# Second layer's first product over pairs of token blocks in 7 block products, with streamed weights and a planned order of instructions

## The chip, the cores and the metric

The kernel runs on one core of one Trainium2 chip, as one launch. The metric is the device time of that launch in microseconds (us), lower is better. Runs of the kernel before: 1168.96 us median of 3 (1168.02 to 1169.71). Five engines work side by side, each through its own instructions in order: TensorE (PE: matmuls, with weight loads as PEld), VectorE (DVE), ScalarE (ACT), GpSimd (POOL) and SyncE (SP, which here only issues DMAs). They wait for each other by semaphores.

## What is computed

Windowed attention gives 3072 tokens x 512 (6 blocks of 512 tokens), then two feed-forward layers follow. With x of shape (3072, 512):

```python
# first layer, d_ff = 1536
gate = 1.0 / (1.0 + np.exp(-(x @ w_gate)))
x = (gate * (x @ w_val)) @ w_out
# second layer, d_ff = 2048
h = x @ w_in
P = a[0] + a[1] * h + a[2] * h**2 + a[3] * h**3
Q = 1.0 + abs(b[0]) * abs(h) + abs(b[1]) * h**2
out = (P / (Q + 1e-06)) @ w_out
```

All data are 32-bit floats. The kernel keeps accuracy by splitting each operand into a high and a low part and adding three matmuls (high-high, high-low, low-high; `TERMS`), so each product of tiles costs three matmuls per 128 rows of contraction. The reciprocal of Q is made as the square of an inverse square root and corrected once.

## The kernel before

**First layer.** The attention of later blocks, the conversion of weights and the first layer are interleaved by a table of steps (`plan`, filled by `at`, run by `runner`). Blocks 0 and 1 take the gate and value products tile by tile (L373). Blocks 2, 3 and blocks 4, 5 are taken as pairs: `quads` calls `quad` (L490), which forms the products of a 2 x 2 arrangement (two blocks, two tiles of features) from 7 block products instead of 8, with differences and sums of x and of the weights made beforehand. Between the quads stand visits (`visit`, `out1`, L575), the products with w_out of an earlier tile; `outs` does the visits of the second block of a pair, whose results were held.

**Conversion.** The weights come as 64-bit words, are staged, decoded by two ScalarE and one VectorE instructions, and split into a high part (ScalarE, L345) and a low part (VectorE, L349). The 32 tiles of the second layer (16 of w_in, 16 of w_out, 512 KB each when split) are converted during the first layer; 28 are stored to HBM and loaded again before the second layer, 4 stay (`DIRECT`). In the second layer all of them are resident.

**Second layer.** For each of 6 blocks and each of 16 tiles f of 128 features: `h2` makes h for 512 tokens (12 matmuls of 512 columns, L618) into one PSUM bank, and then the rational function works on 512-wide tiles; `out2` adds the tile's share to the four accumulators of the block five steps later (12 matmuls, L657):

```python
        nc.scalar.activation(out=t, in_=hp, func=ACTF.Identity, scale=cf[:, 3:4], bias=cf[:, 2:3])
        nc.scalar.activation(out=qq, in_=hp, func=ACTF.Abs, scale=cab[:, 0:1])
        nc.scalar.activation(out=hh, in_=hp, func=ACTF.Square)
        nc.vector.tensor_tensor(out=t, in0=t, in1=hp, op=ALU.mult)
        nc.vector.scalar_tensor_tensor(out=t, in0=t, scalar=cf[:, 1:2], in1=hp, op0=ALU.add, op1=ALU.mult)
        nc.vector.scalar_tensor_tensor(out=qq, in0=hh, scalar=cab[:, 1:2], in1=qq, op0=ALU.mult, op1=ALU.add)
```

`recip2` (two ScalarE instructions, L638 and L639), `ratio2` (three VectorE, L644 to L646) and `split2` (one ScalarE, one VectorE, L560 and L561) follow, one or two steps later. `load_x2` and `split_x2` bring the next block's x from HBM, where the first layer stored it. The order on each engine is the program's, written out in a loop over `steps2`. The first three `h2` run between the last visits of the first layer.

**Buffers.** PSUM has four accumulator banks and four others (`ps`). In SBUF: 20 slots `w` and 8 slots `b` for weights and operands, 4 `x`, 4 `g`, and 14 temporaries `t` of 512 columns.

## Time and profile before

| | before |
|---|---|
| median of the runs | 1168.96 us |
| the profiled execution, its own time | 1168.19 us |
| its span, first to last instruction | 1166.4 us |
| PE busy | 1150.4 us (99%) |
| DVE busy | 865.6 us (74%) |
| ACT busy | 709.3 us (61%) |
| POOL busy | 2.1 us (0%) |
| mean granted TensorE clock | 0.994 of full speed |

The profile is one execution, recorded by the hardware. A busy share is an average over stages with different limits, so a stage is read by itself. Matmuls overlap one another, so the mean duration of one is longer than the distance from one to the next; the same holds, less so, for VectorE and ScalarE. The chain of waits follows the work that ended last back to what released it. A DMA's time to landing is counted from its issue.

### The profile page before, as it was taken

How to read it: one execution, taken by the hardware profiler on the slowest of the kernel's cores; microseconds unless marked ns; L12 is line 12 of the kernel's file. 1: busy time of each engine (PE TensorE's matmuls, PEld its weight loads, DVE VectorE, ACT ScalarE, POOL GpSimd, SP SyncE). 2: the span in 40 equal slices, each digit the busy share in tenths (PEclk: the TensorE clock that was granted, in tenths of full speed). 3: DMA queues.
4: the chain of work that ended last, by engine and by line, in shares of the span. 5: the costliest groups of instructions: out<-in, count | busy, mean ns of one | idle time of the engine just before them, and what ended most of it. 6: DMA issues, size and time to landing. Idle time of an engine off the chain costs nothing.

```text
span 1166.4 us, 19936 instructions
## 1 busy us (share of the span) xinstructions
PE 1150.4 (99%) x7942; PEld 946.7 (81%) x7945; DVE 865.6 (74%) x1342; ACT 709.3 (61%) x1208; POOL 2.1 (0%) x15
## 2 busy tenths in 40 slices
PE   6999999999999999999999999999999999999998
PEld 4788788888888888888888888888888888888887
DVE  5778867874576646556555898898898898888886
ACT  4989566653433365433344876767767767767664
POOL 0000000000000000000000000000000000000000
PEclk8899999999999999999999999999999999999999
DMA  9889799987878668988867620100100100100101
GB/s 371 318 314 336 253 333 382 351 324 280 335 263 295 239 241 320 393 321 284 310 234 312 217 81 10 55 10 10 55 10 10 55 10 10 55 10 1 37 1 36
DMA packets 67356, 218.09 MB, mean 187 GB/s; under 512 B 7488, under 2 KB 7744, under 8 KB 67264
## 3 DMA queue, kind: packets, MB, share of 16 engines
q1 hardware_dynamic: 66688, 215.42, 50.6%
q8 instruction: 62, 1.02, 0.3%
q10 hardware_dynamic: 576, 1.41, 0.3%
q14 instruction: 30, 0.25, 0.1%
HBM read 161.22 MB, written 55.57 MB: 186 GB/s over the span
## 4 chain that ended last, share of the span: by engine, by line
PE 93%; ACT 3%; DMA 2%; DVE 1%; issue 1%; SPq 0%; ACTq 0%; DVEq 0%
PE acc L657 22%; PE h L618 22%; PE p L490 19%; PE acc L575 15%; PE h L373 10%; DMA st<-w_in 2%; PE xp L280 1%; PE sp L220 1%; PE xp L187 1%; PE tp L265 1%; ACT st L310 0%; DMA q<-q_in 0%; ACT st L311 0%; ACT wp L345 0%; PE sp L113 0%
## 5 line engine op out<-in xcount | busy, mean ns | idle before, releaser
L575 PE MATMUL acc<-g,wp 128*128 128x512 f32 x864 | 210.5, 393 | 0.6 <-ACT x2s L591 0.6
L657 PE MATMUL acc<-wp,g 128*128 128x512 f32 x792 | 189.4, 389 | 0.0
L575 PEld LDWEIGHTS acc<-g,wp 128*128 128x128 f32 x864 | 160.2, 188 | 34.9 <-ACT x2s L591 1.0
L657 PEld LDWEIGHTS acc<-wp,g 128*128 128x128 f32 x792 | 148.6, 188 | 30.9
L626 ACT ACTIVATE t<-h,cf 128x512 f32<-128x512 f32 x96 | 74.8, 779 | 148.3 <-PE h L618 148.3
L618 PE MATMUL h<-x,w 128*128 128x512 f32 x648 | 155.5, 389 | 0.0
L618 PEld LDWEIGHTS h<-x,w 128*128 128x128 f32 x648 | 121.6, 188 | 25.3
L373 PE MATMUL h<-x,wp 128*128 128x512 f32 x576 | 139.7, 396 | 2.1 <-ACT x L196 1.5
L490 PE MATMUL p<-b,wpq_s 128*128 128x512 f32 x576 | 138.5, 389 | 0.1
L373 PEld LDWEIGHTS h<-x,wp 128*128 128x128 f32 x576 | 108.9, 191 | 25.3 <-ACT x L196 1.6
L490 PEld LDWEIGHTS p<-b,wpq_s 128*128 128x128 f32 x576 | 108.0, 188 | 22.9 <-DVE v L504 0.5
L618 PE MATMUL h<-x,wp 128*128 128x512 f32 x504 | 121.1, 389 | 0.0
L618 PEld LDWEIGHTS h<-x,wp 128*128 128x128 f32 x504 | 94.6, 188 | 19.7
L629 DVE TENSOR_TENSOR t<-t,h 128x512 f32<-128x512 f32 x96 | 65.9, 686 | 55.4 <-ACT hh L628 54.0
L560 ACT ACTIVATE g<-sg 128x512 fp32r<-128x512 f32 x36 | 22.8, 632 | 104.8 <-DVE sg L520 66.2
L657 PE MATMUL acc<-w,g 128*128 128x512 f32 x360 | 86.5, 389 | 0.0
L657 PEld LDWEIGHTS acc<-w,g 128*128 128x128 f32 x360 | 67.6, 188 | 14.0
L630 DVE SCALAR_TENSOR_TENSOR t<-t,cf,h 128x512 f32<-128x512 f32 x96 | 71.8, 748 | 3.4
L490 PE MATMUL p<-x,wpq_a 128*128 128x512 f32 x288 | 73.2, 389 | 0.0
L631 DVE SCALAR_TENSOR_TENSOR qq<-hh,cab,qq 128x512 f32<-128x512 f32 x96 | 71.7, 747 | 0.0
L645 DVE SCALAR_TENSOR_TENSOR t<-t,cf,y 128x512 f32<-128x512 f32 x96 | 71.6, 746 | 0.0
L644 DVE SCALAR_TENSOR_TENSOR qq<-qq,y 128x512 f32<-128x512 f32 x96 | 65.8, 686 | 7.1 <-ACT y L639 7.1
(120 smaller groups left out, 1506.8 us busy)
## 6 DMA issues: line engine op xcount, KB each, us to landing
st<-w_in SPq DMA_DIRECT2D x62, 512.0 KB, 7.1
wp<-wqa SPq DMA_DIRECT2D x60, 512.0 KB, 7.1
wpq_s<-wqs SPq DMA_DIRECT2D x48, 512.0 KB, 7.5
wpq_a<-wqa SPq DMA_DIRECT2D x36, 512.0 KB, 6.5
wqa<-wp SPq DMA_DIRECT2D x30, 512.0 KB, 8.8
w2d<-wpw SPq DMA_DIRECT2D x28, 512.0 KB, 6.1
v<-v_in SPq DMA_DIRECT2D x24, 512.0 KB, 7.8
wqs<-wps SPq DMA_DIRECT2D x24, 512.0 KB, 5.3
```

The costliest lines, as they stand in the source:

```text
L373: nc.tensor.matmul(pt, lhsT=w[:, a, c : c + P], rhs=x[:, kt, b], start=(h == 0 and kt == 0 and i == 0), stop=(h == 1 and kt == 1 and i == 2),)
L490: nc.tensor.matmul(bank[n], lhsT=wt[:, a, c : c + P], rhs=x[:, kt, b], start=(i < 4 and kt == 0 and t == 0), stop=(kt == 1 and t == 2), sk ...
L560: nc.scalar.activation(out=t[:, 0, 0:n], in_=sg, func=ACTF.Copy)
L575: nc.tensor.matmul(acc[j][d], lhsT=w[:, a, d * P : (d + 1) * P], rhs=g[:, b], start=(f == 0 and i == 0), stop=(f == NF1 - 1 and i == 2),)
L618: nc.tensor.matmul(hp, lhsT=w[:, a, kt * P : (kt + 1) * P], rhs=x[kt // 2][:, kt % 2, b], start=(kt == 0 and i == 0), stop=(kt == KT - 1 a ...
L626: nc.scalar.activation(out=t, in_=hp, func=ACTF.Identity, scale=cf[:, 3:4], bias=cf[:, 2:3])
L629: nc.vector.tensor_tensor(out=t, in0=t, in1=hp, op=ALU.mult)
L630: nc.vector.scalar_tensor_tensor(out=t, in0=t, scalar=cf[:, 1:2], in1=hp, op0=ALU.add, op1=ALU.mult)
L631: nc.vector.scalar_tensor_tensor(out=qq, in0=hh, scalar=cab[:, 1:2], in1=qq, op0=ALU.mult, op1=ALU.add)
L644: nc.vector.scalar_tensor_tensor(out=qq, in0=qq, scalar=QC, in1=y, op0=ALU.add, op1=ALU.mult)
L645: nc.vector.scalar_tensor_tensor(out=t, in0=t, scalar=cf[:, 0:1], in1=y, op0=ALU.add, op1=ALU.mult)
L657: nc.tensor.matmul(acc[j][m], lhsT=g[:, a, m * P : (m + 1) * P], rhs=w[:, b], start=(f == 0 and i == 0), stop=(f == NF2 - 1 and i == 2),)
```

## The change

The second layer takes blocks in 3 pairs and tiles of features in 8 groups of two (`feats`). Per pair and group, 7 block products of 6 matmuls each (`quad2`, `product`, `POS2`) replace the 48 matmuls of four `h2`. The combinations of weights (`COMBS2`) are made during the first layer: 28 tiles of input weights are stored (to `wq2`) for the 16 before, and all 16 output tiles (to `w2o`); none stays resident. Each pair loads them again: per group four loads of input weights (three of 512 KB, one of 256 KB; `load2i`) and four of output weights (512 KB; `load2o`). x of the two blocks is loaded, combined and split into 7 operands (`x_ops`: per pair 8 loads, 8 differences, 14 high and 14 low parts).

The 7 products of a group gather in three PSUM banks: X (taken in turn from two banks), Y and Z. ScalarE copies X out four times as it grows, VectorE adds Y or Z to three of the copies. That gives h of the two tiles for the first block (`hs`) and for the second (`bs`, held in the `x` slots). The rational function (`activation`) runs in passes 1024 wide over the two tiles of a block: five ScalarE instructions each; for the first block (i = 0) six on VectorE, for the second (i = 1) five, its sum b1 h^2 + b0 |h| being made by an accumulating DMA that GpSimd issues, SBUF to SBUF, 512 KB (`q_sum`; `sb` is the square root of b1, made in `second_scalars`).

Visits (`visit2`, 12 matmuls each, as in `out2`) stand two in each group and 16 after the 8 groups of a pair. Accumulators and the banks of the groups change places from pair to pair. Before the first group stand 10 of the first layer's last 14 visits, the other 4 in the first groups' slots.

The order of the second layer comes from a planner in the source (`Plan`): each instruction is a task with an engine, a duration, a latency, and what it reads, writes and takes from the buffer pools. TensorE's tasks keep their order; each other engine takes, whenever it is free in the plan, the ready task with the earliest latest-start. The plan is then emitted as the program order of each engine (`emit`).

The temporaries `t` become 7 buffers of two halves, which come free when both halves are done. `AHEAD` is 3 for 4, `DIRECT` 0 for 4. In the first layer the conversion of second-layer weights stands at other steps (`conv_in`, `conv_out`), with 16 combinations (`comb2`).

The core of the diff:

```diff
-AHEAD = 4
-DIRECT = 4
+AHEAD = 3
+NQ = 8
+NPAIR2 = 3
+DIRECT = 0
+FORDER = [4 * (q // 2) + q % 2 + 2 * i for q in range(8) for i in range(2)]
...
-    tpool = ctx.enter_context(tc.tile_pool(name="t", bufs=14))
+    tpool = ctx.enter_context(tc.tile_pool(name="t", bufs=7))
...
+    def t2w(name):
+        return tpool.tile([P, 2, 512], F32, tag="t", name=name)
+
     def t2(name):
-        return tpool.tile([P, 512], F32, tag="t", name=name)
+        if spare:
+            return spare.pop()[:, 1]
+        t = t2w(name)
+        spare.append(t)
+        return t[:, 0]
...
+    XORDER = ("21", "11", "1", "3", "2", "4", "22")
+    POS2 = (("11", 0), ("21", 1), ("2", 0), ("3", 2), ("1", 0), ("22", 0), ("4", 2))
+
+    def feats(s):
+        f = 4 * (s // 2) + s % 2
+        return f, f + 2
...
+    class Plan:
+        SIZES = {"t": 7, "b": 8, "w": 20, "x": 4, "g": 4}
+        LAT = {"PE": 0.25, "ACT": 0.15, "DVE": 0.15, "POOL": 5.0, "SP": 5.5}
...
+                    for t in queue[:1] if e == "PE" else queue:
+                        if best and best.late <= t.late or e != "PE" and t.late > now - stall + t.window:
+                            continue
+                        if any(
+                            d.start is None or d.start + d.dur + d.lat * (d.eng != e or e != "PE") > now + 1e-9 for d in t.deps
+                        ):
+                            continue
...
+    COMBS2 = {}
+    items = []
+    for fp in range(NF2 // 4):
+        a0, a1, b0, b1 = range(4 * fp, 4 * fp + 4)
+        s0, s1, s2, s3 = (("s", fp, o) for o in range(4))
+        COMBS2[s0] = b0, b1, ALU.add
+        COMBS2[s1] = s0, a0, ALU.subtract
+        COMBS2[s2] = a0, b0, ALU.subtract
+        COMBS2[s3] = a1, s1, ALU.subtract
+        items += [
+            (b1, [(0, b1, fp, 6)], []),
+            (b0, [(0, s0, fp, 4)], [(0, b1)]),
+            (a0, [(0, a0, fp, 0), (0, s2, fp, 3), (1, s1, fp, 2)], [(0, b0), (1, s0), (1, a0), (1, s2)]),
+            (a1, [(0, a1, fp, 1), (0, s3, fp, 5)], [(0, a1), (0, s1), (0, s3)]),
+        ]
+    outs2 = [NF2 + f for f in FORDER]
+    conv_in = [S1 + 1 + i for i in range(4)] + [O1 + 1 + 3 * i for i in range(4)]
+    conv_in += [Q2 + i for i in (0, 1, 2, 3, 5, 6, 7, 8)]
+    conv_out = [4, 5, 7, 17, 19, 20, 22] + [S1 + i for i in range(5, 11)] + [O1 + 2, O1 + 8, Q2 + 4]
...
+        WIN = 11.0
+
+        def load2o(key, f):
+            buf(key, "w", lambda: wpool.tile([P, 2, 512], F32R, tag="w", name="_".join(map(str, key))))
+            t = task(SP, 0.1, lambda: nc.sync.dma_start(out=env[key].bitcast(F32), in_=w2o[f]), (), [key], (), [key], lat=6.0)
+            t.window = WIN
+
+        def load2i(p, s, i):
+            key, n = ("wi", p, s, i), 1 if i == 3 else 2
+            buf(key, "w", lambda: wpool.tile([P, 2, 2, 256], F32R, tag="w", name=f"wi{p}_{s}_{i}"))
+
+            def load():
+                nc.sync.dma_start(out=env[key][:, 0:n].bitcast(F32), in_=wq2[s // 2, s % 2, i, :, 0:n])
+
+            task(SP, 0.1, load, (), [key], (), [key], lat=6.0).window = WIN
...
+            for n, o in enumerate(XORDER):
+                src, dst = pure.get(o, ("xf", p, kt, o)), ("x2", p, o)
+                if o in subs:
+                    x0, x1 = subs[o]
+                    buf(src, "t", lambda src=src: t2("_".join(map(str, src))), 1)
+                    task(
+                        DVE,
+                        0.68,
+                        lambda src=src, x0=x0, x1=x1: tt(out=env[src], in0=env[x0], in1=env[x1], op=ALU.subtract),
+                        [x0, x1],
+                        [src],
+                        [x0, x1],
+                        [src],
+                    )
+                if kt == 0:
+                    buf(dst, "b", lambda dst=dst: b_tile("_".join(map(str, dst)), F32R, [P, 2, 2, 512]))
...
+        def activation(p, s, i):
+            h = (lambda: flat(h_ap(p, s))) if i == 0 else (lambda: flat(b_ap(p, s)))
+            hk = h_key(p, s) if i == 0 else b_key(p, s)
...
+            kt, kq, ku = ((x, p, s, i) for x in "tqu")
+            ky, chain = ku, ("chain", (s, p) if i == 0 else CH(s))
...
+            by_dma = QDMA(i)
+            scale = {"scale": sb[:, 0:1]} if by_dma else {}
+            task(
+                ACT,
+                0.97,
+                lambda: act(out=w(ku), in_=h(), func=ACTF.Square, **scale),
+                [*hr, chain],
+                [ku, kq, kt],
+                [hk],
+                [ku, kq, kt],
+            )
+            task(ACT, 0.97, lambda: act(out=w(kq), in_=h(), func=ACTF.Abs, scale=cab[:, 0:1]), hr, [kq], [hk, kq])
+
+            def q_sum():
+                if by_dma:
+                    nc.gpsimd.dma_start(out=w(kq), in_=w(ku), accum_op=ALU.add)
+                else:
+                    stt(out=w(kq), in0=w(ku), scalar=cab[:, 1:2], in1=w(kq), op0=ALU.mult, op1=ALU.add)
+
+            task(POOL if by_dma else DVE, 1.0 if by_dma else 1.19, q_sum, [ku], [kq], [ku, kq], lat=6.0 if by_dma else None)
...
+            task(
+                ACT,
+                0.97,
+                lambda: act(out=w(ky), in_=w(kq), func=ACTF.Abs_reciprocal_sqrt, bias=qc[:, 0:1]),
+                [kq],
+                [ky],
+                [kq, ky],
+            )
+            task(ACT, 0.97, lambda: act(out=w(ky), in_=w(ky), func=ACTF.Square), (), [ky], [ky])
...
+        def visit2(p, s, i, n):
+            j = 2 * p + i
+            left2.setdefault(j, NF2)
+            first, last = left2[j] == NF2, left2[j] == 1
+            left2[j] -= 1
+            kg, kw = ("G2", p, s, i, n), ("w2o", p, s, i, n)
+            load2o(kw, feats(s)[n])
+
+            def lhs(m, t):
+                a, b = TERMS[t]
+                return env[kg][:, a, m * P : (m + 1) * P], env[kw][:, b]
+
+            split2(p, s, i, n)
+            g = 1 - p % 2 if i == 0 else p % 2
+            products(j, g, True, 0, first, last, lhs, [kg, kg + ("l",), kw], [kg, kw])
...
+            def product(pos):
+                o, n = POS2[pos]
+                kw, kx = ("wi", p, s, pos // 2), ("x2", p, o)
+
+                def mm():
+                    if pos in (0, 1, 3):
+                        env["bank", p, names[n]] = bank(g, tags[names[n]], f"q{p}_{s}_{names[n]}")
+                    wt, x = env[kw][:, pos % 2], env[kx]
+                    if pos == 0:
+                        env[X] = env["bank", p, "X"]
+                    for kt in range(2):
+                        for t, (a, b) in enumerate(TERMS):
+                            nc.tensor.matmul(
+                                env["bank", p, names[n]],
+                                lhsT=wt[:, a, kt * P : (kt + 1) * P],
+                                rhs=x[:, kt, b],
+                                start=(pos in (0, 1, 3) and kt == 0 and t == 0),
+                                stop=(kt == 1 and t == 2),
+                                skip_group_check=True,
+                            )
+
+                writes = [X if n == 0 else (names[n], p)]
...
+                task(PE, 1.36, mm, [kw] + [kx + (kt, b) for kt in range(2) for b in range(2)], writes, [kw, kx])
...
+            product(0)
+            copy(hs[0], hn + (0,), [hk], h_gets())
+            product(1)
+            nxt(0)
+            add(hs[0], hn + (0,), "Y", [hk])
+            product(3)
+            product(2)
+            nxt(1)
+            copy(hs[1], hn + (1,), [hk])
+            visit(0)
+            product(4)
+            copy(bs[1], bn + (1,), [bk], [bk] if s % 2 == 0 else ())
+            add(bs[1], bn + (1,), "Z", [bk])
+            visit(1)
+            product(5)
+            nxt(2)
+            copy(bs[0], bn + (0,), [bk], (), [("Zx", p)])
+            product(6)
+            nxt(3)
+            add(hs[1], hn + (1,), "Z", [hk])
+            activation(p, s, 0)
+            if s < KB:
+                activation(p, s, 1)
...
+        for kt in range(2):
+            x_ops(0, kt)
+        n5 = 10
+        for i, (j, f) in enumerate(todo1):
+            ready1(j, f)
+        for i, (j, f) in enumerate(todo1[:n5]):
+            visit1(j, f)
+        for i in range(4):
+            load2i(0, 0, i)
+        late = list(todo1[n5:])
+        B = [(s, 1, n) for s in range(NQ) for n in range(2)]
+        A = [(s, 0, n) for s in range(NQ) for n in range(2)]
+        TAIL, KB = 6, 8
+        in_slots = 2 * NQ - TAIL
+        rest = A[in_slots:] + B[:-TAIL]
+        order = 'A5B0B1A6B2A7B3B4'
+        rest = []
+        for c, n in zip(order[::2], order[1::2]):
+            rest += [(int(n), 0 if c == "A" else 1, i) for i in range(2)]
+        for p in range(NPAIR2):
+            for s in range(NQ):
+
+                def visit(n):
+                    i = 2 * s + n
+                    if i >= TAIL:
+                        visit2(p, *A[i - TAIL])
+                    elif p:
+                        visit2(p - 1, *B[i - TAIL])
+                    elif late:
+                        visit1(*late.pop(0))
+
+                quad2(p, s, visit)
+            for s in range(KB, NQ):
+                activation(p, s, 1)
+            if p + 1 < NPAIR2:
+                for kt in range(2):
+                    x_ops(p + 1, kt)
+            for v in rest + (B[-TAIL:] if p == NPAIR2 - 1 else []):
+                visit2(p, *v)
+        assert not late
+        T.emit(T.order())
```

## Rows read from the trace of the kernel before

**Rows 1.** The page's busy times: engine, us (share of the span), xinstructions
```profile
PE 1150.4 (99%) x7942; PEld 946.7 (81%) x7945; DVE 865.6 (74%) x1342; ACT 709.3 (61%) x1208; POOL 2.1 (0%) x15
```

**Rows 2.** The chain that ended last, by engine and by line
```profile
PE 93%; ACT 3%; DMA 2%; DVE 1%; issue 1%; SPq 0%; ACTq 0%; DVEq 0%
PE acc L657 22%; PE h L618 22%; PE p L490 19%; PE acc L575 15%; PE h L373 10%; DMA st<-w_in 2%; PE xp L280 1%; PE sp L220 1%; PE xp L187 1%; PE tp L265 1%; ACT st L310 0%; DMA q<-q_in 0%; ACT st L311 0%; ACT wp L345 0%; PE sp L113 0%
```

**Rows 3.** Waits of PE after 300 us: us in total, times, longest
```profile
PE acc L575 <- ACT x2s L591: 0.6, 1, 0.6
```

**Rows 4.** Stretches: PE, PEld, DVE, ACT, POOL busy us, PE clock, DMA share, GB/s
```profile
450.00:500.00 50.00, 49.95 (x220) 40.93 (x219) 28.35 (x44) 20.26 (x36) 0.00 (x0) 1.00 1.02 396
650.00:700.00 50.00, 50.00 (x223) 41.39 (x222) 48.28 (x75) 39.96 (x68) 0.00 (x0) 1.00 0.48 174
700.00:1100.00 400.00, 400.00 (x1766) 331.23 (x1765) 352.29 (x533) 284.15 (x480) 0.00 (x0) 1.00 0.08 24
```

**Rows 5.** Chain of waits, 800 to 830 us: start, us, what
```profile
800.76 2.72 PE h L618 x12
803.48 2.72 PE acc L657 x12
```

**Rows 6.** The same chain, 480 to 520 us
```profile
492.04 9.52 PE p L490 x42
```

**Rows 7.** Groups of instructions by line: busy us, mean ns, idle before
```profile
L618 PE MATMUL h<-x,w 128*128 128x512 f32 x648 | 155.5, 389 | 0.0
...
L618 PE MATMUL h<-x,wp 128*128 128x512 f32 x504 | 121.1, 389 | 0.0
```

**Rows 8.** DVE in order of time, 820 to 832 us: start, us, what
```profile
821.71 0.69 DVE L629 TENSOR_TENSOR t<-t,h 128x512 f32<-128x512 f32 x1 [0.71 <-ACT hh L628]
822.43 0.75 DVE L630 SCALAR_TENSOR_TENSOR t<-t,cf,h 128x512 f32<-128x512 f32 x1
823.10 0.75 DVE L631 SCALAR_TENSOR_TENSOR qq<-hh,cab,qq 128x512 f32<-128x512 f32 x1
823.76 0.68 DVE L644 SCALAR_TENSOR_TENSOR qq<-qq,y 128x512 f32<-128x512 f32 x1
824.37 0.75 DVE L645 SCALAR_TENSOR_TENSOR t<-t,cf,y 128x512 f32<-128x512 f32 x1
```

**Rows 9.** DVE in order of time, 132 to 137 us
```profile
134.13 1.22 DVE L258 TENSOR_TENSOR s<-s,r 128x1024 f32<-128x1024 f32 x1
135.27 1.28 DVE L349 TENSOR_TENSOR wps<-sf,wps 128x512 fp32r<-128x512 f32 x2
```

**Rows 10.** ACT in order of time, 390 to 396 us
```profile
393.03 1.06 ACT L152 ACTIVATE s<-s 128x1024 f32<-128x1024 f32 x1
```

**Rows 11.** ACT in order of time, 820 to 832 us
```profile
827.00 2.07 ACT L668 ACTIVATE o<-acc 128x512 f32<-128x512 f32 x4
```

**Rows 12.** Groups by line, L490
```profile
L490 PE MATMUL p<-b,wpq_s 128*128 128x512 f32 x576 | 138.5, 389 | 0.1
```

**Rows 13.** DMA issues by line: count, KB each, median us to landing
```profile
wp<-wqa SPq DMA_DIRECT2D x60, 512.0 KB, 7.1
...
w<-w2d SPq DMA_DIRECT2D x14, 512.0 KB, 10.2
...
x2f<-x2d SPq DMA_DIRECT2D x24, 256.0 KB, 3.4
```

**Rows 14.** SP's issues in order of time, 595 to 665 us: start, us
```profile
654.47 3.40 SPq L355 DMA_DIRECT2D wp<-w2d  x6
```

**Rows 15.** Groups by line, a converted tile's low and high part
```profile
L349 DVE TENSOR_TENSOR wps<-sf,wps 128x512 fp32r<-128x512 f32 x24 | 15.4, 684 | 0.0
...
L345 ACT ACTIVATE wps<-sf 128x512 fp32r<-128x512 f32 x24 | 13.7, 619 | 0.0
```

More of the change, by code (lines that the diff above doesn't have):

```diff
@@ L957, in visit, with quads @@
             nv += 1
-        def quads(ja, s0, last):
+        def quads(ja, s0):
             for i in range(NF1):
@@ new lines, in fused_kernel, with split, hi, lo @@
+        quads(2, S1)
+        outs(3, O1, lambda i: None)
+        quads(4, Q2)
+        second_scalars()
+        second_scalars()
+        spare.clear()
+        assert not [x for si in plan if si >= O2 for x in plan[si]]
+        T = Plan()
+        env, task, buf = T.env, T.task, T.buf
+        ACT, DVE, PE, SP, POOL = "ACT", "DVE", "PE", "SP", "POOL"
+        act, stt, tt = nc.scalar.activation, nc.vector.scalar_tensor_tensor, nc.vector.tensor_tensor
+        def split(key, src, reads, uses, by_dma):
+            buf(key, "g", lambda: gpool.tile([P, 2, 512], F32R, tag="g", name="_".join(map(str, key))))
+            def hi():
+                act(out=env[key][:, 0], in_=src(), func=ACTF.Copy)
+            def lo():
+                tt(out=env[key][:, 1], in0=src(), in1=env[key][:, 0].bitcast(F32), op=ALU.subtract)
+            def neg():
+                act(out=env[key][:, 1], in_=src(), func=ACTF.Copy, scale=-1.0)
+            def rest():
+                nc.gpsimd.dma_start(out=env[key][:, 1].bitcast(F32), in_=src(), accum_op=ALU.add)
+            if by_dma:
+                task(ACT, 0.62, neg, reads, [key, key + ("l",), ("gorder",)], uses, [key])
+                task(POOL, 1.0, rest, reads, [key + ("l",)], (key, *uses))
+                task(ACT, 0.62, hi, reads, [key], (key, *uses))
+            else:
+                task(ACT, 0.62, hi, reads, [key, ("gorder",)], uses, [key])
+                task(DVE, 0.66, lo, (key, *reads), [key + ("l",)], (key, *uses))
@@ new lines, in products, with mm @@
+        def products(j, g, second, k, first, last, lhs, reads, uses):
+            def mm(ms):
+                for m in ms:
+                    if first:
+                        acc.setdefault(j, {})[m] = bank(g, m, f"acc{int(second)}_{j}_{m}")
+                    for t in range(3):
+                        l, r = lhs(m, t)
+                        nc.tensor.matmul(acc[j][m], lhsT=l, rhs=r, start=(first and t == 0), stop=(last and t == 2))
+            if first:
+                reads = (*reads,)
+            for ms in [[m] for m in range(4)] if last else [list(range(4))]:
+                task(
+                    PE,
+                    0.68 * len(ms),
+                    lambda ms=ms: mm(ms),
+                    reads,
+                    [("accw", j, second, m) for m in ms] + ([("grp", g)] if first else []),
+                    uses,
+                )
+            if last:
+                evict(j, g, second)
@@ new lines, in keep, with h_key, h_ap, h_gets @@
+        def keep(key, pool, make, units=2):
+            buf(key, pool, make, units)
+            T.bufs[key].users += 1
+        keep(("hA",), "b", lambda: b_tile("hA", F32, [P, 4, 512]))
+        kept = set()
+        def h_key(p, s):
+            return ("hA",)
+        def h_ap(p, s):
+            return env[("hA",)][:, 2 * (s % 2) : 2 * (s % 2) + 2]
+        def h_gets():
+            new = () if kept else (("hA",),)
+            kept.add(0)
+            return new
+        def b_key(p, s):
+            return ("hold", p, s // 2)
```

600 lines of the change are left out of this document (449 added, 151 removed).

## The prediction

> **What bounds the kernel now.** I read the busy table first: TensorE is busy for 1150.4 of 1166.4 us [rows 1], so either it is the bound or its row hides waits. The chain that ended last settles it: 93% of it are matmuls, 22% the second layer's first product (L618) and 22% its second product (L657) [rows 2]. The waits of TensorE after 300 us say the same: one wait of 0.6 us, in the first layer [rows 3]. So in the second layer a removed matmul is removed time, as long as nothing else comes late; whatever delays a matmul costs in full.
>
> Next come the stretches by engine. From 700 to 1100 us VectorE is busy 352.3 and ScalarE 284.2 of 400 us, the DMA engines 8% [rows 4]. VectorE has the least room. From 650 to 700 us it is busy 48.3 of 50 us, and TensorE lost nothing in it [rows 4]: a nearly full VectorE can stay hidden if its order fits.
>
> The price of a matmul is not its listed mean of 389 ns, because matmuls overlap; it is the distance in the chain: 12 matmuls of 512 columns in 2.72 us [rows 5], 42 in 9.52 us [rows 6], so 0.2267 us each. By the Trainium skill (TensorE: Matmul & The Clock Gate, Back-to-back issue gap) a stream of weight loads and 512-column matmuls is spaced by about 131 ns; 144 of them would be 18.9 us, and by it the forecast below would be 1155.8 us. The trace's 226.7 ns does not agree with it, and the row decides.
>
> **The change part by part.** Removed: the first product takes 648 + 504 = 1152 matmuls [rows 7], 6 blocks x 16 tiles x 12. After it is 3 pairs x 8 groups x 7 products x 6 = 1008. The second product keeps 3 x 32 x 12 = 1152. So 144 x 0.2267 = 32.6 us go from TensorE. Seen by the group (two tiles for two blocks): 4 x (2.72 + 2.72) = 21.76 us before, 9.52 + 4 x 2.72 = 20.40 us after; 24 x 1.36 = 32.6 us.
>
> VectorE, per group. I price from start to start, since its instructions overlap too: 0.61 us for a 512-wide pass, 0.67 us with a scalar from a tile [rows 8], 1.14 us for a 1024-wide one [rows 9], so 1.14 + 0.06 = 1.20 us with such a scalar. The rational function now runs in 1024-wide passes over two tiles: the first block takes 3 x 1.14 + 3 x 1.20 = 7.02 us, the second 3 x 1.14 + 2 x 1.20 = 5.82 us, as its sum for the denominator goes to a DMA. Then 3 additions of products (1.83), 4 low parts of g (2.44), and 22 passes per pair for x differences and low parts (22 x 0.61 / 8 = 1.68). Together 18.8 us of 20.4, 92%. Before, 88% was hidden [rows 4].
>
> ScalarE, per group: 10 wide passes at 1.06 us [rows 10], 4 copies of a product out of PSUM, 4 high parts, one eviction and 1.75 high parts of x at 0.52 (four evictions took 2.07 us [rows 11]): 10.6 + 10.75 x 0.52 = 16.2 us, 79%. Neither engine bounds by its sum. What can cost is the order: the second block's products land in one bank, which ScalarE must copy before TensorE adds the next product to it. Between a product and the next on that bank stand two other products or a visit, so 2.72 us of cover. The first layer's block products already work like that, on L490; the costliest of its rows shows 576 matmuls with 0.1 us idle [rows 12]. Lower end per group 0; upper end one 1.14 us vector pass in front of an urgent addition that uses up the cover each time, 24 x 1.14 = 27.4 us. I take 2 us, near the row of L490, which has the same pattern.
>
> The seams. Before the first group, x of blocks 0 and 1 must be loaded, combined and split: 22 vector and 14 scalar passes, beside 10 splits of the first layer's last block. Ten visits (27.2 us) cover it. Two rounds of loads at 3.4 us [rows 13] plus issue, each followed by 11 x 0.61 = 6.7 us, and 6.1 us of other splits: about 6.8 + 13.4 + 6.1 = 26.3 us plus a few issues. It just fits; what is late next is the first group's last operand. At the two pair seams the cover is 16 visits, 43.5 us, for the same work. The nearest row for a seam is the 0.6 us wait [rows 3]; I take 1.5 us for each of three, 4.5 us; from below 0, from above the whole of one 6.7 us round each, 20 us.
>
> DMA of the second layer. Before, all its weights were resident; now each group loads 1.75 MB of input weights and 2 MB of output weights: 3.75 MB in 20.4 us, about 190 GB/s, where 396 GB/s ran from 450 to 500 us [rows 4]. 512 KB land in 7.1 us under the first layer's load and in 10.2 us in a saturated stretch [rows 13]. The planner starts a load up to 11 us before its latest start and counts 6 us of landing, so it has up to 17 us. SP issues about 10 per group at 0.57 us (six in 3.40 us [rows 14]): 5.7 of 20.4 us. It waits in order for free buffers, but its stores of outputs and loads of x stand in the planned order among them. Cost 0; if loads were late by 10.2 - 7.1 us once per group, 74 us, which I hold unlikely at half the rate of that stretch.
>
> The accumulating DMA is new: POOL's queue adds u to q in SBUF, 512 KB, once per group. POOL has nothing else queued. ScalarE's reciprocal root waits for it, and behind that wait stand, in ScalarE's order, the copies that TensorE needs. No row shows such a transfer. From below it is the 256 KB load's 3.4 us, from above 14.2 us, twice the 7.1 us of a 512 KB load because two operands are read [rows 13]. I take 7.1 us, the row of the same size, which is what the planner counts (1.0 + 6.0): cost 0.
>
> The first layer. 28 tiles of input weights instead of 16 are stored, all 16 output tiles too (44 stores for 28), and 16 combinations made: 28 more vector passes, 12 more scalar ones, each about 0.68 and 0.62 us [rows 15], 19 and 7 us. They lie over the 330 us from 270 to 600 us, where VectorE is busy about 60% (28.4 of 50 us in [rows 4]); cost 0. Without that cover the 19 us would show. The stores and loads on SP move past first-layer loads and wait for low parts; loads of output weights run five visits ahead, 13.6 us. Half of the temporary tiles now share a buffer with a neighbour and come free together: I give nothing for it.
>
> **The sum**, against the profiled execution: 1168.2 us (span 1166.4 plus 1.8 around it) - 32.6 + 4.5 + 2.0 = 1142.1, so 1142 us. That execution is 0.8 us below the median of the runs, 1168.96, well inside what matters here. The floor is 1168.2 - 32.6 = 1135.6 us, with no new wait.
>
> **The rivals.**
> 1. VectorE sets the pace, still faster. For it: priced by listed means (1.22 for 1024 wide [rows 9] and so on) its group comes to about 20.4 us, equal to TensorE's, and it waits for ScalarE now and then, 0.71 us each [rows 8]. Against: 48.3 of 50 us busy hurt nothing. With one such wait per group and no slack, 24 x 0.75 = 18 us: about 1160 us.
> 2. The accumulating DMA lands late: the slower case. Place: ScalarE, at the reciprocal root of each second block, 24 times. ScalarE has 20.4 - 16.2 = 4.2 us per group to absorb, so from a landing of 7.1 + 4.2 = 11.3 us it holds TensorE, and from 11.3 + 32.6 / 24 = 12.7 us the kernel is slower. At 14.2 us: 24 x 2.9 = 70 us, 1135.6 + 70 = 1205 us. For it: it reads two operands. Against: the second layer's engines are far from saturated. The Trainium skill (Collectives: The Full Stack, The bandwidth ceiling: the fold count) says that a transfer that adds needs two source reads and so runs at about half a copy's rate. By the Trainium skill (DMA: Bandwidth & Descriptors, Anatomy of one DMA) a DMA issued from POOL takes about 2 us plus its bytes at 436 GB/s, an estimate of 4.4 us for 1 MB read: by that rule this rival falls. No run here shows either.
> 3. The first layer pays. The stretch from 450 to 500 us is already saturated (DMA share 1.02) [rows 4]; just before it the change adds 5 stores and 2 loads, 3.7 MB, 9.4 us at 396 GB/s. If weights of the block products come late by that, 1142 + 9 = 1151 us. Against: in that stretch TensorE lost 0.05 us, and loads are issued ahead.
> 4. The products go but the time does not: the weight slots (20) hold streamed weights and three wide temporaries per activation, so that loads wait for slots. Same price as a late load, 1.36 us per group cancelling the gain: about 1168 us.
>
> **How the numbers follow.** Forecast 0.56, of itself 1135 to 1150 us; rival 1 0.16; rival 2 0.13; rival 3 0.09; rival 4 0.06. A difference under 0.2% (2.3 us) cannot be told from none here. Faster: the forecast, most of 1 and 3 and a milder 2: 0.78. Same: 0.04, from 4. Slower: most of 2, parts of 1 and 4: 0.18. Range 1134 to 1170 us: 0.02 below, about 0.16 above.
>
> **What would show it.** The first product's line in the profile after has 1008 matmuls, 42 in 9.52 us; TensorE's busy time falls to about 1118 us and its idle time after 600 us stays under 8 us. VectorE is busy about 95% of the second layer by listed means. Rival 1 shows as TensorE waits released by VectorE additions, rival 2 as ScalarE waits on POOL's DMA with 11 us or more to landing, rival 3 as TensorE idle before 600 us, rival 4 as TensorE waits on DMA loads of weights. A saving of less than 30 us in TensorE's busy time would make the count or its price wrong.

## The result, and the profile after

The changed kernel takes 1151.74 us (median of 4 runs, 1150.83 to 1152.35), the kernel before 1168.71 us beside it (4 runs). The ratio is 0.9854 with the 95% interval 0.9836 to 0.9871. So it is faster by 17.0 us (1.5%), where 26.2 were forecast from the profiled execution's own time (1168.2 to 1142); the time lies in the range. The profiled execution after took 1152.35 us, its span is 1150.6 us.

The page's busy times and its groups of the second layer, answering to [rows 1] and [rows 7] (line, engine, operation, count | busy us, mean ns | idle before):

```profile
PE 1122.4 (98%) x7798; PEld 920.3 (80%) x7801; DVE 877.0 (76%) x1184; ACT 736.6 (64%) x1097; POOL 23.1 (2%) x39
...
L1282 PE MATMUL acc<-w2o,G 128*128 128x512 f32 x1152 | 268.7, 389 | 0.0
...
L1567 PE MATMUL q_X<-x,wi 128*128 128x512 f32 x576 | 146.9, 390 | 2.4 <-ACT hb L1587 1.5
...
L1567 PE MATMUL q_Z<-x,wi 128*128 128x512 f32 x288 | 73.1, 389 | 0.0
```

With 144 more on q_Y, L1567 has 1008 matmuls, for 1152 before. TensorE's busy time fell by 28.0 us, and its idle time grew from 16.0 to 28.2 us. Where both happened is seen when the span is cut at the same work in both kernels: at the first and last row of the first layer's block products of blocks 2 and 3, and of blocks 4 and 5. The five stretches are: up to the block products of blocks 2 and 3; these; the visits of block 3; the block products of blocks 4 and 5; the rest, which is nearly all second layer. First before, then after (length, then busy us of PE, PEld, DVE, ACT, POOL, granted clock, DMA share, GB/s):

```profile
257.80:404.46 146.66, 146.66 (x1131) 120.93 (x1130) 91.06 (x133) 58.80 (x90) 0.49 (x3) 1.00 0.75 272
404.46:457.46 53.00, 52.30 (x719) 43.42 (x718) 28.87 (x44) 30.27 (x56) 0.00 (x0) 1.00 0.72 265
457.46:597.95 140.49, 140.44 (x619) 115.84 (x618) 76.97 (x117) 51.71 (x90) 0.00 (x0) 1.00 0.87 316
597.95:1166.40 568.45, 564.56 (x2491) 467.15 (x2489) 478.51 (x724) 391.45 (x661) 0.00 (x0) 1.00 0.16 58
```

```profile
257.32:408.70 151.38, 147.85 (x1131) 120.83 (x1130) 99.05 (x147) 66.38 (x104) 0.49 (x3) 1.00 0.80 300
408.70:466.74 58.04, 52.58 (x720) 43.55 (x719) 34.44 (x53) 35.28 (x66) 0.00 (x0) 1.00 0.80 293
466.74:610.77 144.03, 142.01 (x619) 116.92 (x618) 86.05 (x132) 52.00 (x91) 0.00 (x0) 0.99 0.85 315
610.77:1150.60 539.83, 533.64 (x2347) 439.61 (x2345) 467.54 (x529) 405.65 (x525) 21.01 (x24) 1.00 0.72 231
```

The rest is 28.6 us shorter, TensorE's busy time in it 30.9 us. The three stretches of the first layer, with the same number of matmuls, are longer by 4.7, 5.0 and 3.5 us. Together with 0.5 us at the start this is the whole difference of the spans, 15.8 us.

In the second layer TensorE hardly waits. Its waits from 600 us to the end of the changed kernel (us in total, times, longest), the stretches that answer to [rows 4], and the chain that answers to [rows 6]:

```profile
PE q_X L1567 <- ACT hb L1587: 1.5, 1, 1.5
PE q_X L1567 <- ACT hA L1587: 0.8, 2, 0.7
```

```profile
700.00:800.00 100.00, 100.00 (x443) 82.81 (x442) 96.53 (x109) 82.79 (x107) 3.48 (x4) 1.00 0.78 251
800.00:900.00 100.00, 100.00 (x443) 82.81 (x442) 93.62 (x99) 82.58 (x101) 5.23 (x6) 1.00 0.78 242
900.00:1000.00 100.00, 99.79 (x437) 81.34 (x436) 88.97 (x103) 70.80 (x96) 3.46 (x4) 1.00 0.75 247
1000.00:1100.00 100.00, 100.00 (x443) 82.80 (x442) 95.41 (x100) 85.25 (x104) 4.34 (x5) 1.00 0.74 231
```

```profile
994.50 1.36 PE q_X L1567 x6
995.86 1.36 PE q_Z L1567 x6
```

Six matmuls stand 1.36 us apart, 42 are 9.52 us, as forecast. VectorE is busy 93.6% of 700 to 1100 us and TensorE still loses 0.2 us there.

In the first layer TensorE's waits in the changed kernel, 255 to 660 us:

```profile
PE xp L292 <- ACT xs L279: 3.9, 2, 2.8
PE p L502 <- ACT xs L538: 2.0, 1, 2.0
PE p L502 <- issue: 1.2, 1, 1.2
PE xp L292 <- issue: 1.0, 1, 1.0
PE sp L232 <- issue: 0.9, 1, 0.9
PE p L502 <- DVE v L516: 0.7, 1, 0.7
PE p L502 <- DVE u L516: 0.7, 1, 0.7
PE acc L587 <- ACT at L603: 0.6, 1, 0.6
```

The last of these was there before, alone [rows 3]. The largest group stands in the visits of block 3. L279 is ScalarE's copy of the transposed attention weights, which the product with v (L292) needs. ScalarE in order of time shows why it was late: it stood 4.18 us for a load at the head of its queue, and ran late from there on; at 457.88 us it stood for another. The first fence is ScalarE, the second TensorE (start, us, what, idle before):

```profile
427.75 0.63 ACT L572 ACTIVATE g<-gh 128x512 fp32r<-128x512 f32 x1
432.56 0.65 ACT L322 ACTIVATE st<-st 128x512 f32<-128x512 f32 x1 [4.18 <-DMA x2d<-at]
...
441.95 0.58 ACT L279 ACTIVATE xs<-tp 128x512 f32<-128x512 f32 x1
...
457.88 0.66 ACT L322 ACTIVATE st<-st 128x512 f32<-128x512 f32 x1 [1.84 <-DMA st<-w_in]
```

```profile
442.59 1.14 PE L292 MATMUL xp<-xs,v 64*64 64x32 f32 x64 [2.76 <-ACT xs L279]
```

L322 is the first pass over a staged tile of second-layer weights, and its load is L313 on SP. At 432.56 the profile names another transfer (`x2d<-at`) as what came last; that the wait was for the staging load follows from the times below. SP's issues in that stretch, and SP's longest wait up to 430 us:

```profile
411.15 0.75 SPq L313 DMA_DIRECT2D st<-w_in  x1
422.25 0.32 SPq L864 DMA_DIRECT2D w2o<-wpw  x1
...
424.51 0.37 SPq L313 DMA_DIRECT2D st<-w_in  x1
...
450.37 0.37 SPq L867 DMA_DIRECT2D wq<-wpw_('s', 1, 0)_5126  x1
...
451.34 0.79 SPq L313 DMA_DIRECT2D st<-w_in  x1
```

```profile
SPq L864 <- DVE wpw L859: 14.0, 2, 10.3
```

From 411.9 to 422.2 us SP stood at a store of a converted output tile (L864), which waited for VectorE's low part (L859). The staging load behind it went out at 424.51, with a median of 8.0 us to landing for the three such loads there, and ScalarE came to it at 428.4. It happened again later: from 440.9 to 450.4 us SP stood at L867, again for a low part (9.4 us), and the load behind it, issued at 451.34, is the one that ScalarE stood for at 457.88.

### The profile page after: what moved, and what is told of

Read it like the earlier page. It is cut to its first block, busy times and chain, and to the rows that moved or that the text cites. A ratio compares the mean times of both kernels' runs of the same rounds, so it can differ in the third digit from the quotient of the medians.

```text
span 1150.6 us, 19963 instructions
## 1 busy us (share of the span) xinstructions
PE 1122.4 (98%) x7798; PEld 920.3 (80%) x7801; DVE 877.0 (76%) x1184; ACT 736.6 (64%) x1097; POOL 23.1 (2%) x39
## 5 line engine op out<-in xcount | busy, mean ns | idle before, releaser
L1282 PE MATMUL acc<-w2o,G 128*128 128x512 f32 x1152 | 268.7, 389 | 0.0
L1282 PEld LDWEIGHTS acc<-w2o,G 128*128 128x128 f32 x1152 | 216.1, 188 | 45.3 <-DVE G L1235 0.4
L1567 PE MATMUL q_X<-x,wi 128*128 128x512 f32 x576 | 146.9, 390 | 2.4 <-ACT hb L1587 1.5
L502 PE MATMUL p<-b,wpq_s 128*128 128x512 f32 x576 | 140.1, 392 | 2.6 <-issue 1.2
L385 PE MATMUL h<-x,wp 128*128 128x512 f32 x576 | 139.4, 396 | 2.1 <-ACT x L208 1.5
L1567 PEld LDWEIGHTS q_X<-x,wi 128*128 128x128 f32 x576 | 107.7, 188 | 26.7 <-ACT hb L1587 2.4
L385 PEld LDWEIGHTS h<-x,wp 128*128 128x128 f32 x576 | 108.7, 190 | 25.3 <-ACT x L208 1.6
L1567 PE MATMUL q_Z<-x,wi 128*128 128x512 f32 x288 | 73.1, 389 | 0.0
L1482 ACT ACTIVATE u<-q,qc 128x1024 f32<-128x1024 f32 x48 | 54.4, 1146 | 20.1 <-DMA q<-u 18.2
L1567 PEld LDWEIGHTS q_Z<-x,wi 128*128 128x128 f32 x288 | 54.1, 188 | 11.3
L1491 DVE SCALAR_TENSOR_TENSOR q<-q,u 128x1024 f32<-128x1024 f32 x48 | 58.5, 1221 | 5.4 <-ACT u L1487 5.1
L1499 DVE SCALAR_TENSOR_TENSOR t<-t,cf,u 128x1024 f32<-128x1024 f32 x48 | 61.2, 1279 | 0.0
L572 ACT ACTIVATE g<-c 128x512 fp32r<-128x512 f32 x21 | 13.3, 632 | 72.0 <-DVE c L532 69.8
L322 ACT ACTIVATE st<-st 128x512 f32<-128x512 f32 x62 | 41.3, 666 | 8.2 <-DMA x2d<-at 4.2
L1587 ACT ACTIVATE hb<-q_X 128x512 f32<-128x512 f32 x48 | 28.2, 588 | 27.8 <-PE q_X L1567 27.8
```

The lines of the kernel that those rows point to most:

```text
L322: nc.scalar.activation(out=y, in_=y, func=ACTF.Prelu, scale=2.0**-112, alpha=2.0**32)
L385: nc.tensor.matmul(pt, lhsT=w[:, a, c : c + P], rhs=x[:, kt, b], start=(h == 0 and kt == 0 and i == 0), stop=(h == 1 and kt == 1 and i == 2),)
L502: nc.tensor.matmul(bank[n], lhsT=wt[:, a, c : c + P], rhs=x[:, kt, b], start=(i < 4 and kt == 0 and t == 0), stop=(kt == 1 and t == 2), sk ...
L1282: nc.tensor.matmul(acc[j][m], lhsT=l, rhs=r, start=(first and t == 0), stop=(last and t == 2))
L1482: lambda: act(out=w(ky), in_=w(kq), func=ACTF.Abs_reciprocal_sqrt, bias=qc[:, 0:1]),
L1491: lambda: stt(out=w(kq), in0=w(kq), scalar=QC, in1=w(ky), op0=ALU.add, op1=ALU.mult),
```

## The experiments

The names in the expectations: T1 is that the added conversion work of the first layer delays what TensorE needs, T2 that it is the paired temporaries, T3 that loads come later (`AHEAD`); after the first four runs T1 became theory B (the number of passes), against theory A (the wait for a staging load, by its place in SP's queue). The stretches of the profiled execution of each run, in us, cut as above, and the medians of the runs:

| kernel | to blocks 2, 3 | block products 2, 3 | visits of block 3 | block products 4, 5 | rest | median |
|---|---|---|---|---|---|---|
| before | 257.8 | 146.7 | 53.0 | 140.5 | 568.5 | 1168.71 |
| after | 257.3 | 151.4 | 58.0 | 144.0 | 539.8 | 1151.74 |
| e1_single_t | 257.9 | 151.6 | 60.0 | 141.5 | 538.5 | 1151.26 |
| e2_ahead4 | 257.3 | 153.9 | 61.4 | 140.1 | 538.5 | 1152.86 |
| e3_no_combos | 258.7 | 149.1 | 59.5 | 140.1 | 538.9 | 1148.63 |
| e4_sum_on_dve | 258.5 | 151.6 | 60.7 | 140.8 | 540.3 | 1152.59 |
| e5_early_staging | 258.1 | 151.5 | 53.4 | 140.6 | 538.6 | 1143.62 |
| e6_off_visits | 258.0 | 153.2 | 55.3 | 140.1 | 540.1 | 1147.48 |
| e6b_more_in_last | 259.5 | 151.5 | 54.2 | 140.4 | 538.5 | 1145.65 |
| e7_no_conv_in_visits | 258.5 | 149.8 | 54.2 | 140.1 | 538.9 | 1143.01 |
| e8_pair_max_first | 257.0 | 151.0 | 58.8 | 142.2 | 539.2 | 1149.86 |
| e9_both | 257.9 | 150.7 | 54.2 | 140.1 | 538.5 | 1143.54 |

**e1_single_t**: temporaries as before, 14 single ones.

```diff
-    tpool = ctx.enter_context(tc.tile_pool(name="t", bufs=7))
+    tpool = ctx.enter_context(tc.tile_pool(name="t", bufs=14))
...
-        if spare:
-            return spare.pop()[:, 1]
-        t = t2w(name)
-        spare.append(t)
-        return t[:, 0]
+        return tpool.tile([P, 512], F32, tag="t", name=name)
```

> The changed kernel with 14 separate temporaries instead of 7 buffers of two halves; nothing else. The first layer of the changed kernel takes 12.8 us longer than before: 4.7 in the block products of blocks 2 and 3, 5.0 in the visits of block 3, 3.5 in the block products of blocks 4 and 5. Theory T1 (the added conversion passes stand on ScalarE and VectorE ahead of copies that TensorE waits for): no change, 1151 us within 1.5. Theory T2 (halves that come free only together make later passes wait): most of the 12.8 us comes back, about 1140 us. Theory T3 (more DMA traffic, or weights asked for later with AHEAD 3): no change.

1151.26 us, ratio to before 0.9845 (0.9817 to 0.9874). The time did not move: T2 falls.

**e2_ahead4**: loads of block-product weights four ahead.

```diff
-AHEAD = 3
+AHEAD = 4
```

> The changed kernel with AHEAD 4 as before; nothing else. T3 in its form that the block products' weights are asked for too late: 3 to 8 us back, 1143 to 1148 us. T1 and T2: no change, 1151 us within 1.5.

1152.86 us, 0.9859 (0.983 to 0.9887), the visits even 3.4 us longer: T3 falls in this form.

**e3_no_combos**: the 16 combinations are not formed, and the splits of 16 tiles into high and low parts are left out with them. Plain tiles are stored in their places, so the stores and loads are as many.

```diff
...
-            (b1, [(0, b1, fp, 6)], []),
-            (b0, [(0, s0, fp, 4)], [(0, b1)]),
-            (a0, [(0, a0, fp, 0), (0, s2, fp, 3), (1, s1, fp, 2)], [(0, b0), (1, s0), (1, a0), (1, s2)]),
-            (a1, [(0, a1, fp, 1), (0, s3, fp, 5)], [(0, a1), (0, s1), (0, s3)]),
+            (b1, [(0, b1, fp, (6, 4))], [(0, b1)]),
+            (b0, [], [(0, b0)]),
+            (a0, [(0, a0, fp, (0, 2, 3))], [(0, a0)]),
+            (a1, [(0, a1, fp, (1, 5))], [(0, a1)]),
```

> Leaves out the 16 combinations of second-layer weights and the splits of 16 tiles (12 combined ones, 4 plain ones that the change stores only in combinations), and stores plain tiles in their places, so loads and stores are as many as in the changed kernel; the output is not the reference's. T1: 8 to 12 us come back in the three stretches of the first layer, 1140 to 1144 us, and the second layer keeps its 538.5 us. T2: part of it, since 16 temporaries fewer are held, but then the run with separate temporaries shows it too. T3: no change.

1148.63 us, 0.9823 (0.9794 to 0.9851). The medians differ by 3.1 us from the changed kernel's, but the intervals overlap. In the profile 2.3 of the 4.7 us come off the block products of blocks 2 and 3: of the four waits of TensorE there, those at 335 and 353 us are gone. The visits stay at 59.5 us. So the combinations and splits are half of the loss in that stretch, and a small part of the whole; T1 had expected 8 to 12 us.

**e4_sum_on_dve**: the second block's sum for the denominator on VectorE again, no accumulating DMA.

```diff
-            return i == 1
+            return False
```

> The changed kernel with the sum for the second block's denominator on VectorE too, no accumulating DMA; the planner makes its order anew. By the prediction's own prices VectorE then has 18.8 + 1.2 = 20.0 us per group of 20.4. If VectorE has the room that these prices give it, the second layer grows by 0 to 5 us. If it is already the pace in the order as planned (rival 1), by 12 us or more.

1152.59 us, 0.9856 (0.9828 to 0.9885), the rest 0.5 us longer. From 700 to 1100 us VectorE is busy 96.2% there, and TensorE loses 0.15 us. The pass that goes back to VectorE, 1.2 us per group, costs nothing that can be told: rival 1 of the prediction falls, and the accumulating DMA is worth as little.

**e5_early_staging**: the staging loads of the six tiles converted in the visits of block 3 are issued two steps earlier. Nothing else changes.

```diff
-        at(s0, conv2_load, u, s0 not in used and (S1 <= s0 < O1 or Q2 <= s0) and lag == 1)
+        at(s0 - 2 if O1 <= s0 < Q2 else s0, conv2_load, u, s0 not in used and (S1 <= s0 < O1 or Q2 <= s0) and lag == 1)
```

> Only the six staging loads of the weights that are converted during the visits of block 3 are issued two steps earlier. Theory A (ScalarE stands 4.2 us at the head of its queue for a staging load, and the x parts behind it come late): that wait goes, the stretch of the visits falls from 58 to about 54 us and the time to about 1147 us. Theory B (the number of conversion passes of ScalarE and VectorE in that stretch is what delays the x parts): the wait goes, but the stretch stays within 1.5 us of 58 and the time at 1150 to 1152.

1143.62 us, 0.9781 (0.9766 to 0.9795), and the interval lies wholly below the changed kernel's. The visits are back at 53.4 us, and the block products of blocks 4 and 5 at 140.6. SP, ScalarE and TensorE of this kernel, at the places shown above:

```profile
408.39 0.33 SPq L313 DMA_DIRECT2D st<-w_in  x1
...
411.52 0.38 SPq L367 DMA_DIRECT2D wp<-wqa  x1
421.94 0.32 SPq L864 DMA_DIRECT2D w2o<-wpw  x1
```

```profile
427.94 0.69 ACT L322 ACTIVATE st<-st 128x512 f32<-128x512 f32 x1
```

```profile
439.43 1.14 PE L292 MATMUL xp<-xs,v 64*64 64x32 f32 x64
```

SP stands as long at the same store, from 411.9 to 421.9 us, but the load is now ahead of it. ScalarE takes L322 without a wait, and so does TensorE its products at 439.43 (of the wait of 1.1 us at 455 us, 0.5 us stays); from 400 to 480 us ScalarE has no wait on a load left. The passes are all still there (ScalarE busy 736.6 us in both). So theory A holds: neither the work nor the transfer cost the time, but the load's place behind a store that waits. A had put the time at about 1147 us; the 3.4 us beyond that came back in the block products of blocks 4 and 5.

What the wait drags behind it is in the next stretch. The changed kernel, then this one, from 470 to 480 us (columns as for the stretches above):

```profile
470.00:480.00 10.00, 7.98 (x29) 5.90 (x28) 6.55 (x10) 3.54 (x8) 0.00 (x0) 0.83 1.03 405
```

```profile
470.00:480.00 10.00, 9.87 (x44) 8.19 (x45) 2.85 (x6) 4.94 (x9) 0.00 (x0) 1.00 1.04 409
```

After ScalarE's second stand TensorE waited 2.0 us at 474 us for a copy (`xs L538`, made 7.0 us into the stretch, in e5 4.8 us), and the granted clock is 0.83 of 2.4 GHz there, part of it thus at 1.2 GHz; without the waits it is 1.00. The stretch lost 3.5 us, 1.6 of it as longer busy time.

In e1 to e4 and in e8 the loss stands one stretch earlier. They have the wait at 442 us too (2.2 to 3.5 us), but there the clock fell right behind it: it is 0.94 over their visits, where the changed kernel's execution has 1.00. That is why their visits take 59 to 61 us and their block products of blocks 4 and 5 only 140 to 142. In e3, with the one wait of 2.2 us at 441 us:

```profile
440.00:450.00 10.00, 8.78 (x144) 7.62 (x145) 5.27 (x9) 6.62 (x13) 0.00 (x0) 0.66 1.03 398
```

**e6_off_visits** and **e6b_more_in_last**: the six conversions stand at other steps, all of the work kept.

```diff
-    conv_in = [S1 + 1 + i for i in range(4)] + [O1 + 1 + 3 * i for i in range(4)]
-    conv_in += [Q2 + i for i in (0, 1, 2, 3, 5, 6, 7, 8)]
-    conv_out = [4, 5, 7, 17, 19, 20, 22] + [S1 + i for i in range(5, 11)] + [O1 + 2, O1 + 8, Q2 + 4]
+    conv_in = [S1 + 1 + i for i in range(8)] + [Q2 + i for i in (0, 1, 2, 3, 5, 6, 7, 8)]
+    conv_out = [4, 5, 7, 17, 18, 19, 20, 21, 22, 23, S1, S1 + 9, S1 + 10, Q2 + 2, Q2 + 4, Q2 + 6]
```

> No weight is converted during the visits of block 3: the six units move to the steps before and after, all of the work is kept. Theory B (conversion passes in the visits delay the x parts): the visits fall from 58 to 53 or 54 us, and with the clock that the wait costs the time comes to 1143 to 1146 us, if the steps that take the units have room. Rival (the first layer's passes have no free place: what leaves the visits shows in the block products beside them): visits shorter by 4 us or more, the stretches beside it longer by as much, time 1150 to 1153.

1147.48 us, 0.9813 (0.9798 to 0.9827), between what B and its rival expected: the visits fall to 55.3 us, the block products of blocks 2 and 3 grow to 153.2. For e6b the new lines are:

```diff
+    conv_in = [S1 + 1 + i for i in range(4)] + [Q2 + i for i in (0, 0, 1, 2, 3, 3, 4, 5, 6, 6, 7, 8)]
+    conv_out = [4, 5, 7, 17, 18, 19, 20, 21, 22, 23] + [S1 + i for i in range(5, 11)]
```

> As the kernel that keeps conversions out of the visits of block 3, but with the block products of blocks 2 and 3 relieved as well: the units go to the last block products of the first layer, up to two in a step. Theory B: visits 53 to 54 us, time 1143 to 1146 us. Rival (no free place): the block products of blocks 4 and 5 grow from 144 to 148 us or more and the time stays at 1149 to 1153.

1145.65 us, 0.9793 (0.9777 to 0.981), visits 54.2 us, block products of blocks 4 and 5 140.4. Both take the loads away from SP's wait as well as the passes, so they don't tell A from B; they show that the last block products have room for these passes, the earlier ones less.

**e7_no_conv_in_visits**: the six conversions in the steps from O1 to Q2 are left out; other tiles are stored in their places.

```diff
...
+    def skipped(s0):
+        return O1 <= s0 < Q2
...
+        if skipped(s0):
+            continue
```

> The conversion of the six units that fall in the visits of block 3 is left out (four input tiles of the second layer and two output tiles; other tiles are stored in their places, so the output is not the reference's). Theory B: the visits fall to 53 or 54 us, the wait of 3.9 us and the lower clock after it go, the time is 1143 to 1146 us. Rival (the x parts of that block are late by themselves, behind the sums of the seven products): the stretch stays at 57 us or more and the time at 1149 or more.

1143.01 us, 0.9775 (0.9755 to 0.9794). Without the conversion the kernel is no faster, within the intervals, than e5, which keeps it. So the passes themselves cost nothing there; B, which forecast this run as well, is not needed.

**e8_pair_max_first**: in the block products' steps, bit passes and combinations after the row maxima of the attention. **e9_both**: the same with the earlier staging loads.

```diff
-                run(conv2_bits, comb2, pair_sum)
-                run(done2)
+                run(pair_sum)
                 if i != 1:
                     visit(run)
+                run(conv2_bits, comb2)
+                run(done2)
```

> The changed kernel with one order altered: in the steps of the first layer's block products VectorE takes the second layer's bit passes and combinations after the row maxima of the attention instead of before. Theory (block products of blocks 2 and 3 grew from 146.7 to 151.4 us since VectorE reaches the maxima late, 1.2 us of wait at 335, and the rest of it in the products' additions): 149 us there, as without the combinations, the time 1149 to 1150 us. Rival (the waits there are the additions' own and move along): 151 us there and 1151 to 1152 us.

> Earlier staging loads for the visits of block 3, and the maxima of the attention ahead of bit passes and combinations in the block products. Theory: the two gains add, 1143.6 less 2 to 2.5, 1141 to 1142 us. Rival (the maxima's order brings nothing): 1143 to 1144 us.

e8 took 1149.86 us, 0.9835 (0.9821 to 0.9848), e9 1143.54 us, 0.9785 (0.9771 to 0.9798), the same as e5. The time of e8 is the one that its theory gave, but not for its reason: the block products of blocks 2 and 3 take 151.0 us, not 149, and its interval overlaps the changed kernel's. In the changed kernel VectorE and TensorE stood like this around 335 us:

```profile
333.27 0.69 DVE L836 TENSOR_TENSOR c<-c,c 128x512 f32<-128x512 f32 x1
333.88 0.68 DVE L259 TENSOR_REDUCE m<-sp 128x8 f32<-128x512 f32 x1
334.60 0.69 DVE L260 TENSOR_TENSOR s<-sp,m 128x512 f32<-128x512 f32 x1
```

```profile
335.39 1.86 PE L502 MATMUL p<-b,wpq_s 128*128 128x512 f32 x7 [1.17 <-issue]
```

TensorE resumes when L260, behind a combination (L836), has ended; the profile names no releaser, so this is read from the times. In e9 this wait is gone, but another grew from 0.7 to 1.1 us. TensorE's waits of e9 from 257 to 409 us, in order of time:

```profile
352.50 1.65 PE L502 MATMUL p<-b,wpq_s 128*128 128x512 f32 x6 [1.10 <-DVE v L516]
...
379.65 1.66 PE L502 MATMUL p<-b,wpq_s 128*128 128x512 f32 x6 [0.72 <-DVE u L516]
...
386.37 0.30 PE L232 MATMUL sp<-k,q 64*32 64x64 f32 x4 [0.96 <-issue]
```

The stretch keeps 150.7 of 151.4 us: the wait moved on for the most part, and the rival expectation of e9 is what came.

## Why the prediction was right, and where it was mis-sized

**Right: the price and the count.** 1008 matmuls, 42 in 9.52 us. TensorE's busy time fell by 30.9 us in the rest (32.0 in e5), against 32.6 forecast. The prediction's test, less than 30 us of saving over the whole span, would have called the count or the price wrong, as the saving was 28.0; the test was too coarse, since the first layer's busy time grew by 3.0 us (restarts and the lower clock).

**Right: no engine bounds the second layer.** VectorE was put at 92% and is at 93.6%, ScalarE at 79% and is at 80.4%. The seams and the order of the groups were given 4.5 and 2.0 us; measured are 2.3 us of listed waits after 600 us, all but 0.2 at the first group, and TensorE's idle time in the rest is 6.2 us, under the 8 us that the prediction allowed. Rival 1 falls with that and with e4.

**Right: the accumulating DMA.** It was taken as 7.1 us to landing. The trace after shows, for its line, and for ScalarE's waits on it from 600 us on:

```profile
DMA to landing us min/median/max: 4.6/6.5/11.5
```

```profile
ACT u L1482 <- DMA q<-u: 18.2, 13, 4.8
```

Its longest landing reaches the 11.3 us from which rival 2 was to begin, but the median is 6.5, and of ScalarE's 18.2 us of waits one reached TensorE: ScalarE stood 1.64 us up to 968.80, its copy of a product came behind that, and TensorE waited 0.16 us for the copy, up to 970.49. So the mechanism of rival 2 is there, at next to no cost. By the Trainium skill (Collectives: The Full Stack, The bandwidth ceiling: the fold count) the reduce step of a ring of three or more ranks, which reads two sources, runs at about half the rate of the copying step; the page says this of rings, not of a transfer within one core, to which the prediction carried it over. Beside plain loads of 512 KB that landed in 4.8 and 5.9 us (medians of the two kinds of second-layer weights), 6.5 us does not show a half rate here.

**Mis-sized: the step "The first layer ... cost 0".** It costs 13.3 us (4.72 + 5.04 + 3.54). The prediction named the piece that failed, "The stores and loads on SP move past first-layer loads and wait for low parts", and gave it nothing; what it set against the added work was VectorE's free 40%. But free time on VectorE is not cover for a wait that holds SP's queue. Such waits were there before: SP stood up to 11.7 us at a store for a low part between 400 and 440 us, and ScalarE once waited 3.2 us for a staging load, at 458 us, in the block products, where it cost TensorE nothing. In the changed order the late load falls in the visits, where ScalarE soon owes TensorE copies. e5 removes 8.1 us of the median with that one line.

The errors partly cancel. The rest came out 2.5 us better than forecast (28.6 us shorter, where 32.6 - 4.5 - 2.0 = 26.1 were forecast), and the start 0.5 us; the first layer took 13.3 us for 0. That makes the 10.3 us between 1142.1 and the profiled execution's 1152.35. So the time missed the 1135 to 1150 us of the forecast itself by 1.7 us, and it is the width of the range, which was there for the rivals, that held it. Two slips in the prediction's sums change nothing: rival 1 prices a wait of 0.71 us at 0.75, and 3.7 MB at 396 GB/s are 9.3 us, not 9.4.

**Rival 3 had the place and nearly the size** (TensorE idle before 600 us, 1151 us; it was given 0.09), with another mechanism: it expected weights of the block products to be late by the amount of traffic. No wait of TensorE on a load is listed between 255 and 660 us.

With the early loads the time is 1143.6 us, 1.6 above the forecast. That nearness is luck in part: the waits of the second layer were priced 4.2 us too dear, and 4.8 us remain in the block products of blocks 2 and 3.

**What stays open** are those 4 to 5 us. Four waits of 0.7 to 1.2 us are listed there. Two stand behind VectorE's additions of products (L516); one, at 335 us, went with the order of e8 and e9, but most of the time stayed; without the combinations (e3) this one and one of the two are gone.

The last, at 386 us, stands in the middle of 128 small matmuls of one kind and names nothing it waited for; it is in every version here at 0.8 to 1.2 us (0.3 in e7) and not in the kernel before. The trace suggests what it was, though no run tested it. In all of them it comes after the 124th of these matmuls (125th where a record is missing), so it follows the program and not the time. The profile's DMA queue for instructions (q8) starts a transfer of 16 KB at 384.17 us in the changed kernel, 2.4 us before the wait's end, and 2.3 to 2.6 us before it in the others. That is 0.03 us ahead of the first of these matmuls; in the kernel before it starts at 379.74 us, 1.4 us ahead of them, and nothing waits. So this looks like a wait for the program's own instructions. In the 5 us before the transfer the DMA engines' share is 1.03 in the changed kernel, 0.95 in e7 and 0.85 in the kernel before; whether that traffic delays it is not shown.

The best version run is e5, 1143.62 us, faster than both kernels; e9 adds nothing to it that can be measured.

## What to carry to other kernels

Price a moved or added store by what stands behind it in its queue. Follow it to the first load, the engine that has that load at its head, and what this engine owes to the bound engine: here 10.3 and 9.4 us on SP became 4.2 and 1.8 us on ScalarE and then 2.8, 1.1 and 2.0 us on TensorE. A busy share of 60% hides work, but no wait in an ordered queue. Issue loads by when their consumer needs them and ahead of stores that wait for a late producer; that one line gave nearly half as much again as the whole change.

## What the runs showed of the hardware that was not expected

A listed wait of TensorE costs more than its length. In the block products of blocks 2 and 3 of the changed kernel four waits add up to 3.5 us idle, and the busy time of the same 1131 matmuls grew by 1.2 us at a granted clock of 1.00: 0.3 us more for each wait. The other runs agree. Against the 146.66 us of the kernel before, which has no wait there, two waits (e3) make it 147.25 us, three (e7) 147.56, five (e6) 148.14 and six (e2) 148.45; in e8 and e9, with three, it is 0.4 us for each. It is seen in the rows too: six matmuls in a stream are 1.36 us from start to start but 1.52 us to the modelled end, and 1.65 us after a wait. The idle time is counted from that modelled end, 0.16 us late, and the row after it is 0.13 us longer.

A wait of 2 to 3 us cost as much again in clock in some runs. Over the visits of block 3 TensorE is busy 52.3 to 52.7 us where the granted clock is 1.00, and 54.7 to 55.9 us in the five runs where it is 0.94, with the same matmuls. In e3 it was 0.66 from 440 to 450 us, part of it thus at 1.2 GHz, with a wait of 2.2 us at 441. In the changed kernel it stayed at 1.00 behind the wait of 2.8 us at 442 us and was 0.83 from 470 to 480 us, with the wait of 2.0 us at 474. Behind which wait it fell was not the same from run to run, and the table's stretches move with it.
